# Linear attention and an MLP on one core: maxima of q and k subtracted on GpSimd for batches 4 to 7, with these batches' steps in other slots

## The chip, the cores and the metric

The kernel runs on one core of one Trainium2 chip. The core has five engines, each with its own instruction queue that is worked off in order: TensorE (PE, with its weight loads as PEld), VectorE (DVE), ScalarE (ACT), GpSimd (POOL) and SyncE (SP), which here issues most of the DMAs. The metric is the device time of one execution in microseconds (us), of which the median over several runs is taken.

## What is computed

The reference is a linear attention, followed by an MLP with a leaky activation:

```python
q_s = q - np.max(q, axis=-1, keepdims=True)          # q, k, v: 8 x 8 x 576 x 64
q_s = np.exp(q_s)
q_s = q_s / (np.sum(q_s, axis=-1, keepdims=True) + 1e-09)
k_s = k - np.max(k, axis=2, keepdims=True)
k_s = np.exp(k_s)
k_s = k_s / (np.sum(k_s, axis=2, keepdims=True) + 1e-09)
kv = np.einsum('bhsd,bhse->bhde', k_s, v)
a = np.einsum('bhsd,bhde->bhse', q_s, kv)

x = a.transpose(0, 2, 1, 3).reshape(4608, 512)
h = x @ w_in                                         # 512 x 2048
g = np.maximum(0.01 * h, h)
out = g @ w_out                                      # 2048 x 512
```

## The kernel before

**Tiles.** The 4608 tokens are nine tiles of 512, and the attention has eight batches of 576 tokens. Batch b's attention has to be ready ahead of the tile that first needs its tokens, so the attention of later batches is worked in between the matmuls of earlier tiles. The last two tiles are treated in another way (fewer products from sums of weights, which DVE and GpSimd form in `out_weight_sums` and `in_weight_sums`, L825); the change doesn't touch them.

**A plain tile** has two layers on PE. Layer 1 (L563) is 16 groups of four matmuls of 128x512; each group fills one PSUM bank `ph` out of a pool of six, and ACT's `leaky` (L572, out `gj`) empties it. Layer 2 (L584) is four token blocks of 16 matmuls; each block fills one of two banks `pout`, and ACT copies it to `out_sb` (L578), from where SP stores it. The six banks are also those of the attention.

**Slots.** The order of everything else is written by hand: `at(t, u, ...)` hangs functions in slot u of tile t. Slots 0 to 15 come after the groups of layer 1, slots 16 to 31 in layer 2, one after each four matmuls; a slot of 32 or more counts on into the next tile. What a slot issues is appended to the queues of its engines, so the slots fix each engine's order.

**The steps of a batch b**, with the names and lines that the profile shows. q and k are 128 partitions x 2304 elements (4 pairs of heads, 9 rows, 64), in f32, in a pool of six buffers shared with v:

- `load_all` (L84): SP's DMAs of k, q and v.
- `k_tree` (L160): DVE, four maxima over the rows of k, out `t` and `kmax`; in `k_max` of the plan.
- `k_allmax` (L167 to L190): DVE, the maximum over the partitions, out `kall`.
- `k_sub` (L198): k less its maximum, on the engine that it is given; `k_exp` (L206): ACT, out `ke`.
- `q_max` (L245): DVE; `q_sub` (L304): q less its maximum, on the engine that it is given; `q_exp` (L312): ACT, out `qe`.
- `q_sum` (L321, with the reciprocal L323) and `q_norm` (L328): DVE, together `q_ready`; `q_turn` (L551): a transposing DMA in SP's queue, out `qX`.
- `v_cast` (L216 on ACT, L218 on GpSimd): v to bf16, out `vb`.
- `attend_kv(b)`: PE interleaves the product of keys and values of batch b + 1 (L341) with the attention of batch b (L479) in six banks `pokv` and `po`. DVE's `kd_make(b + 1)` (L361, L362) follows, and then ACT's six copies to `xT` (L500), the last two of which read the banks `pokv` that `kd_make` reads, too. `kd` of b + 1 is what attends the next batch.

`k_tree`, `k_allmax`, `q_max`, `q_sum` and `q_norm` are DVE's in all batches from 2 on; GpSimd subtracts only for parts of batches 0 to 2 in the kernel before. `q_front(b, t, u)` of the plan stands for `q_max` and `q_sub(nc.vector, ...)`.

Of the kernel before, what the change touches and what calls it, by code (L numbers as in the profile page):

```python
# [26 lines left out]
def kernel(  # L27
# [9 lines left out]
    nc = tc.nc  # L37
# [52 lines left out]
    ALLH, ALLR = slice(0, HL), slice(0, R)  # L90
# [71 lines left out]
    def k_allmax(b):  # L162
        k_lanes(b)
        k_cross(b)

    def k_lanes(b):
        nc.vector.transpose(  # L167
            out=st[b]["kmaxT"], in_=st[b]["kmax"].rearrange("p h d -> p (h d)")
        )
        st[b]["m2"] = m2 = small_pool.tile([P, CB, 2], FP32, name="m2")  # L170
        nc.vector.tensor_reduce(
            out=m2[:, :, 0],
            in_=st[b]["kmaxT"].rearrange("p (c j) -> p c j", j=32),
            axis=AX.X,
            op=ALU.max,
        )

    def k_cross(b):
        m2 = st[b]["m2"]
        for a in range(4):  # L180
            o = a ^ 1
            nc.vector.tensor_reduce(
                out=m2[32 * o : 32 * o + 32, :, 1],
                in_=m2[32 * a : 32 * a + 32, :, 0:1],
                axis=AX.X,
                op=ALU.max,
            )
        m = small_pool.tile([P, CB], FP32, name="m")
        nc.vector.tensor_reduce(out=m, in_=m2, axis=AX.X, op=ALU.max)
        nc.vector.transpose(  # L190
            out=st[b]["kall"].rearrange("p h d -> p (h d)"),
            in_=m.unsqueeze(2).to_broadcast([P, CB, 32]),
        )

    def k_sub(eng, b, hs):
        ks = st[b]["k"][:, hs]
        n = hs.stop - hs.start
        eng.tensor_tensor(  # L198
            out=ks,
            in0=ks,  # L200
            in1=st[b]["kall"][:, hs].unsqueeze(2).to_broadcast([P, n, R, D]),
            op=ALU.subtract,
        )

    def k_exp(b, hs):
        nc.scalar.activation(  # L206
            out=st[b]["ke"][:, :, hs].rearrange("p r h d -> p h r d"),
            in_=st[b]["k"][:, hs],
            func=AF.Exp,
        )  # L210
# [10 lines left out]
    def q_cols(b, rs, hs):  # L221
        if b != 1:
            return st[b]["qe"][:, rs, hs]
        blocks = XE if rs.start else XH[hs.start // 2]
        return qe1[:, blocks].rearrange("p n c -> p (n c)").rearrange(
            "p (r h d) -> p r h d", h=hs.stop - hs.start, d=D
        )

    def turned(name):
        return qT_pool.tile([P, XE.stop, P], BF16, name=name, tag="qT")  # L230
# [11 lines left out]
    def q_max(b, rs, hs=ALLH):  # L242
        n, m = rs.stop - rs.start, hs.stop - hs.start
        st[b]["qmax", rs.start, hs.start] = o = small_pool.tile([P, HL, n], FP32, name="qmax")[:, 0:m]
        nc.vector.tensor_reduce(out=o, in_=st[b]["q"][:, hs, rs], axis=AX.X, op=ALU.max)  # L245
# [55 lines left out]
    def q_sub(eng, b, rs, hs=ALLH):  # L301
        n, m = rs.stop - rs.start, hs.stop - hs.start
        qs = st[b]["q"][:, hs, rs]
        eng.tensor_tensor(  # L304
            out=qs,
            in0=qs,
            in1=st[b]["qmax", rs.start, hs.start].unsqueeze(3).to_broadcast([P, m, n, D]),
            op=ALU.subtract,
        )

    def q_exp(b, rs, hs=ALLH):
        nc.scalar.activation(  # L312
            out=q_cols(b, rs, hs).rearrange("p r h d -> p h r d"),
            in_=st[b]["q"][:, hs, rs],
            func=AF.Exp,
        )
# [19 lines left out]
    def kv_quads(b, gg, outs, rs=ALLR):  # L336
        for r in range(R)[rs]:
            for hp in range(2):
                for hh in range(2):
                    rows = slice(hh * L, (hh + 1) * L)  # L340
                    nc.tensor.matmul(  # L341
                        outs[hh][hp * D : (hp + 1) * D, 0 : D + 1],
                        lhsT=st[b]["ke"][rows, r, 2 * gg + hp],
                        rhs=vb2[b % 2][rows, r, gg, hp, 0 : D + 1],
                        start=(r == 0),
                        stop=(r == R - 1),
                    )
# [139 lines left out]
    def attend(b, ggs, rows, pool=psB_pool, tag=BANK_TAG):  # L487
        n = (rows.stop - rows.start) * L
        ps = [pool.tile([P, len(ggs), n], FP32, name="po", tag=tag) for _ in range(2)]
        for i, gg in enumerate(ggs):  # L490
            cross(b, gg, [ps[hp][:, i] for hp in range(2)], rows)
        st[b]["po", ggs, rows.start] = ps
# [11 lines left out]
    def attend_kv(b, rows=R7, rest=RE):  # L504
        n = 2 * (rest.stop - rest.start) * L
        both = [psB_pool.tile([P, n + 2 * (D + 2)], FP32, name="pokv", tag=BANK_TAG) for _ in range(2)]
        ps = [a[:, 0:n].rearrange("p (g c) -> p g c", g=2) for a in both]
        st[b + 1]["pkv"] = pkv = [a[:, n:].rearrange("p (g d) -> p g d", g=2) for a in both]
        part = lambda gg, r0, r1: kv_quads(b + 1, gg, [pkv[hh][:, gg] for hh in range(2)], slice(r0, r1))
        part(0, 0, 6)  # L510
        attend(b, (0,), rows)
        part(0, 6, R)
        part(1, 0, 3)
        attend(b, (1,), rows)
        part(1, 3, R)
        for gg in range(2):
            cross(b, gg, [ps[hp][:, gg] for hp in range(2)], rest)
        keep = [lambda gg=gg, hp=hp: x_keep(nc.scalar, b, (gg,), rows, hp) for gg in range(2) for hp in range(2)]
        st[b]["po", (0, 1), rest.start] = ps
        kd_make(b + 1)  # L520
        for fn in keep:
            fn()
        for hp in range(2):
            x_keep(nc.scalar, b, (0, 1), rest, hp)
# [23 lines left out]
    def q_turn(b, rs=ALLR):  # L548
        if rs.start == 0:
            st[b]["qX"] = turned("qX")[:, 0 : 2 * R]  # L550
        nc.sync.dma_start_transpose(  # L551
            out=st[b]["qX"][:, 2 * rs.start : 2 * rs.stop],
            in_=st[b]["qe"][:, rs].rearrange("p r h d -> p (r h d)"),
        )
# [40 lines left out]
    def at(t, u, *fns):  # L595
        while t > 0 and u >= 32:
            t, u = t + 1, u - 32
        hooks.setdefault((t, u), []).extend(fns)
# [7 lines left out]
    def load_all(b, order="kqv"):  # L606
        for name in order:
            cuts = [(H0, ALLR), (H1, ALLR)] if b == B - 1 or (b, name) in ((B - 2, "q"), (B - 2, "v")) else [(ALLH, ALLR)]
            st[b][name] = load(dict(q=q, k=k, v=v)[name], b, f"{name}_raw", cuts)
# [134 lines left out]
    def q_front(b, t, u):  # L744
        at(t, u, lambda: q_max(b, ALLR), lambda: q_sub(nc.vector, b, ALLR))
# [19 lines left out]
    def k_max(b, t, u):  # L765
        at(t, u, lambda: k_begin(b), lambda: q_begin(b), lambda: k_tree(b, ALLH))

    def k_less(b, t, u):
        at(t, u, lambda: k_allmax(b), lambda: k_sub(nc.vector, b, ALLH))

    def q_ready(b, t, u):
        at(t, u, lambda: q_sum(b, ALLR), lambda: q_norm(b, ALLR))

    def casts_act(b, *slots):
        for gg, (t, u) in enumerate(slots):
            at(t, u, lambda gg=gg: v_cast(nc.scalar, b, gg))

    q_front(4, 2, 20)
    k_max(5, 2, 28)
    at(2, 30, lambda: q_exp(4, ALLR))  # L780
    q_ready(4, 2, 30)
    casts_act(5, (3, 4), (3, 8))
    at(3, 8, lambda: q_turn(4), lambda: load_all(6, "kvq"))
    k_less(5, 3, 8)
    at(3, 14, lambda: k_exp(5, ALLH))
    q_front(5, 3, 14)
    at(3, 18, lambda: attend_kv(4))
    k_max(6, 3, 19)
    at(3, 20, lambda: q_exp(5, ALLR))
    q_ready(5, 3, 20)  # L790
    casts_act(6, (3, 28), (3, 30))
    at(3, 22, lambda: load_all(7, "kv"))
    at(3, 31, lambda: q_turn(5), lambda: load_all(7, "q"))
    k_less(6, 3, 31)
    at(4, 4, lambda: k_exp(6, ALLH))
    q_front(6, 4, 4)
    at(4, 9, lambda: q_exp(6, ALLR))
    k_max(7, 4, 9)
    q_ready(6, 4, 9)
    casts_act(7, (4, 16), (4, 16))  # L800
    at(4, 17, lambda: attend_kv(5))
    k_less(7, 4, 18)
    at(4, 18, lambda: q_turn(6))
    at(4, 22, lambda: k_exp(7, ALLH))
    q_front(7, 4, 24)
    at(4, 28, lambda: attend_kv(6))
    at(5, 0, lambda: q_exp(7, ALLR))
    at(5, 0, lambda: out_weight_tiles(), lambda: out_weight_sums("v1"))
    q_ready(7, 5, 0)
    at(5, 9, lambda: q_turn(7))  # L810


    TA, TB = NT - 2, NT - 1
# [706 lines left out]
```

## Time and profile before

| what | us |
|---|---|
| median of three runs (276.83 to 277.02) | 276.88 |
| the profiled execution | 277.08 |
| its span in the profile | 275.0 |
| PE busy | 266.7 |
| DVE busy | 225.1 |
| ACT busy | 184.5 |
| GpSimd (POOL) busy | 78.6 |

Times in the views are microseconds from the start of the span, durations of one instruction in groups are nanoseconds. A row of a timeline gives start, duration, engine, line, operation, out<-in, shape and count; a row of grouped instructions gives the count, then busy time and mean of one, and behind the second bar the engine's idle time ahead of them with what ended it. A timeline's row of several instructions runs from the start of the first to the end of the last.

### The profile page before, as it was taken

To read this page: it belongs to the slowest core of one execution; us is meant where nothing else is said; L and a number is where in the kernel's file an instruction comes from. 1 tells how busy PE (TensorE), PEld (TensorE's weight loads), DVE (VectorE), ACT (ScalarE), POOL (GpSimd) and SP (SyncE) were. 2 spreads that over 40 slices of the span, in tenths; PEclk is the share of its full clock that TensorE was granted. 3 is DMA by queue.
4 is the path that set the end of the run, shared out by engine and by line. 5 is a ranking of instruction groups with operands and counts; after the bars stand their busy time and mean duration, and the time that the engine had idled before them with its cause. 6 is when DMAs were issued, how large, how long until landed. Compare 5 with 4: busy or idle time off the path is not lost.

```text
span 275.0 us, 5446 instructions
## 1 busy us (share of the span) xinstructions
PE 266.7 (97%) x2090; PEld 162.8 (59%) x2114; DVE 225.1 (82%) x330; ACT 184.5 (67%) x336; POOL 78.6 (29%) x97
## 2 busy tenths in 40 slices
PE   8799999999999999999999999999999999999994
PEld 3378644444444554454445444466676777889994
DVE  2995995999999999978999995989945757669962
ACT  3977573785389368986699569657746767984241
POOL 2866470149103000000000910000002999950000
PEclk9999999999999999999999999999999999999999
DMA  6999999987997699597991631400033000025254
GB/s 233 338 210 318 245 274 261 391 278 238 241 380 281 76 334 341 108 384 226 374 228 49 126 79 38 86 4 0 2 76 76 0 4 0 0 52 117 64 115 115
DMA packets 40569, 46.48 MB, mean 169 GB/s; under 512 B 18912, under 2 KB 24288, under 8 KB 40544
## 3 DMA queue, kind: packets, MB, share of 16 engines
q1 hardware_dynamic: 36720, 41.56, 51.2%
q0 software_dynamic: 3504, 4.20, 8.8%
q10 hardware_dynamic: 320, 0.39, 0.4%
q8 instruction: 16, 0.26, 0.4%
q14 instruction: 9, 0.07, 0.1%
HBM read 36.70 MB, written 9.44 MB: 168 GB/s over the span
## 4 chain that ended last, share of the span: by engine, by line
PE 93%; DVE 3%; DMA 2%; issue 1%; ACT 0%; SPq 0%
PE ph L563 35%; PE pout L584 25%; PE pout L1095 10%; PE pq L1344 10%; PE pp L1063 9%; DMA k_raw<-in_k_dram 2%; PE po L479 2%; DVE t L160 1%; PE pokv L341 1%; PE pkv L341 1%; PE pkv L419 0%; DVE k_raw L410 0%; ACT ke L206 0%; DVE kmax L160 0%; DVE kd L434 0%
## 5 line engine op out<-in xcount | busy, mean ns | idle before, releaser
L563 PE MATMUL ph<-xT,w_in_sb 128*128 128x512 bf16 (+1 forms) x503 | 98.9, 352 | 0.5
L563 PEld LDWEIGHTS <-w_in_sb 128*128 128x128 bf16 x512 | 49.5, 98 | 46.0 <-issue 0.2
L584 PE MATMUL pout<-w_out_sb,gj 128*128 128x512 bf16 x309 | 70.1, 379 | 1.1 <-issue 0.8
L572 ACT ACTIVATE gj<-ph 128x512 bf16<-128x512 f32 x88 | 49.2, 606 | 14.0 <-PE ph L563 13.0
L584 PEld LDWEIGHTS <-gj 128*128 128x128 bf16 x320 | 30.6, 98 | 36.2 <-issue 0.4
L825 POOL TENSOR_TENSOR t<-w_in_sb 128x256 fp32r<-128x256 bf16 x16 | 11.1, 693 | 62.1 <-ACT vb L216 62.1
L321 DVE TENSOR_REDUCE qsum<-qe 128x36 f32<-128x2304 bf16 (+5 forms) x13 | 20.0, 1542 | 4.7 <-ACT qe L312 4.5
L206 ACT ACTIVATE ke<-k_raw 128x2304 bf16<-128x2304 f32 (+2 forms) x13 | 18.0, 1383 | 6.1 <-DVE k_raw L198 5.7
L328 DVE TENSOR_TENSOR qe<-qe,qrec 128x2304 bf16<-128x2304 bf16 (+5 forms) x13 | 21.5, 1656 | 0.4
L578 ACT COPY out_sb<-pout 128x512 f32<-128x512 f32 x16 | 9.5, 591 | 17.9 <-PE pout L584 13.4
L245 DVE TENSOR_REDUCE qmax<-q_raw 128x36 f32<-128x2304 f32 (+5 forms) x13 | 20.0, 1537 | 0.4 <-DMA q_raw<-in_q_dram 0.4
L312 ACT ACTIVATE qe<-q_raw 128x2304 bf16<-128x2304 f32 (+5 forms) x13 | 17.2, 1326 | 4.2 <-POOL q_raw L304 3.2
L198 DVE TENSOR_TENSOR k_raw<-k_raw,kall 128x1152 f32<-128x1152 f32 (+2 forms) x10 | 18.0, 1820 | 0.3
L572 ACT ACTIVATE xT<-ph 128x512 bf16<-128x512 f32 x24 | 13.9, 600 | 6.3 <-PE ph L563 6.0
L304 POOL TENSOR_TENSOR q_raw<-q_raw,qmax 128x512 f32<-128x512 f32 (+3 forms) x7 | 11.8, 1680 | 20.7 <-DVE qmax L245 19.2
L1260 DVE COPY u<-pp 128x512 f32<-128x512 f32 x8 | 5.5, 691 | 13.5 <-PE pp L1063 13.5
L500 ACT CAST xT<-po 128x448 bf16<-128x448 f32 (+3 forms) x31 | 13.2, 510 | 3.4 <-PE po L479 3.4
L1289 POOL COPY gate<-u 128x1 f32<-128x1 f32 x1 | 0.2, 187 | 52.5 <-DVE u L1066 52.5
L218 POOL CAST vb<-v_raw 128x1152 bf16<-128x1152 f32 x7 | 9.8, 1435 | 17.3 <-DMA v_raw<-in_v_dram 17.3
L1063 PE MATMUL pp<-s,t 128*128 128x512 f32 x48 | 13.9, 398 | 0.0
L304 DVE TENSOR_TENSOR q_raw<-q_raw,qmax 128x2304 f32<-128x2304 f32 (+1 forms) x6 | 13.2, 2203 | 0.2
L825 POOL TENSOR_TENSOR t<-w_in_sb,t 128x256 fp32r<-128x256 bf16 x16 | 13.1, 818 | 0.6
(169 smaller groups left out, 441.9 us busy)
## 6 DMA issues: line engine op xcount, KB each, us to landing
out_dram<-out_sb SPq DMA_DIRECT2D x60, 128.0 KB, 3.0
k_raw<-in_k_dram SPq DMA_DIRECT2D x8, 576.0 KB, 5.7
v_raw<-in_v_dram SPq DMA_DIRECT2D x8, 576.0 KB, 7.6
q_raw<-in_q_dram SPq DMA_DIRECT2D x4, 1152.0 KB, 9.3
v_raw<-in_v_dram SPq DMA_DIRECT2D x4, 1152.0 KB, 11.4
k_raw<-in_k_dram SPq DMA_DIRECT2D x4, 1152.0 KB, 6.2
q_raw<-in_q_dram SPq DMA_DIRECT2D x4, 576.0 KB, 6.9
w_in_sb<-in_moe_w_in_dram POOLq DMA_DIRECT2D x7, 256.0 KB, 6.8
```

What stands on the lines that cost most here:

```text
L198: eng.tensor_tensor(out=ks, in0=ks, in1=st[b]["kall"][:, hs].unsqueeze(2).to_broadcast([P, n, R, D]), op=ALU.subtract,)
L245: nc.vector.tensor_reduce(out=o, in_=st[b]["q"][:, hs, rs], axis=AX.X, op=ALU.max)
L304: eng.tensor_tensor(out=qs, in0=qs, in1=st[b]["qmax", rs.start, hs.start].unsqueeze(3).to_broadcast([P, m, n, D]), op=ALU.subtract,)
L321: nc.vector.reduce_sum(out=qsum, in_=q_cols(b, rs, hs), axis=AX.X)
L328: nc.vector.tensor_tensor(out=qes if out is None else out, in0=qes, in1=st[b]["qrec", rs.start, hs.start].unsqueeze(3).to_broadcast([P, n, ...
L563: nc.tensor.matmul(ph, lhsT=w_in_sb[:, cb, j * P : (j + 1) * P], rhs=xT[:, cb, c0 : c0 + n], start=(cb == 0 and first), stop=(cb == NB - 1 ...
L572: nc.scalar.activation(out=o, in_=ph, func=AF.Prelu, alpha=LEAKY_SLOPE)
L584: nc.tensor.matmul(pout, lhsT=g_sb[j // 2][:, j % 2, tsub * P : (tsub + 1) * P], rhs=w_out_sb[:, j, os], start=(j == 0), stop=(j == NF - 1),)
L825: eng.tensor_tensor(out=late[o], in0=a, in1=b, op=ALU.subtract)
L1063: nc.tensor.matmul(ps, lhsT=w(c), rhs=a(c), start=(first and c == 0), stop=(c == 1), skip_group_check=True)
L1095: nc.tensor.matmul(ps[:, i], lhsT=a(m)[:, i * P : (i + 1) * P], rhs=w(m), start=(first and m == 0 and i == 0), stop=(m == NH - 1 and i == ...
L1344: nc.tensor.matmul(ps[i], lhsT=a(m)[:, i * P : (i + 1) * P], rhs=w(m), start=(first and m == 0 and (each or i == 0)), stop=(m == NH - 1 an ...
```

## The change

The q and k subtractions of batches 4 to 7 go to GpSimd, except that of k of batch 4, which stays on DVE. `q_less(b)` replaces `q_front(b)`: the same `q_max` on DVE, then `q_sub` on GpSimd. `k_all(b)` replaces `k_less(b)`: the same `k_allmax` on DVE, then `k_sub` on GpSimd. All slots of these batches but some are new: the maxima of k of batch 5 are issued at slot (2,22) rather than (2,28), so ahead of `attend_kv(3)` at (2,27) rather than behind it; those of batches 6 and 7 at (3,13) and (3,27) rather than (3,19) and (4,9). `attend_kv(4)` and `attend_kv(5)` keep their slots, `attend_kv(6)` goes from (4,28) to (4,23), and the last transposition of q from (5,9) to (4,25). The loads of k and v of batch 6 come ahead of the transposition of q of batch 4. Lines of the changed kernel behind the plan are four further on (L825 is L829).

```diff
-    def k_less(b, t, u):
-        at(t, u, lambda: k_allmax(b), lambda: k_sub(nc.vector, b, ALLH))
-
@@
-    q_front(4, 2, 20)
-    k_max(5, 2, 28)
+    def q_less(b, t, u):
+        at(t, u, lambda: q_max(b, ALLR), lambda: q_sub(nc.gpsimd, b, ALLR))
+
+    def k_all(b, t, u):
+        at(t, u, lambda: k_allmax(b), lambda: k_sub(nc.gpsimd, b, ALLH))
+
+    q_less(4, 2, 20)
+    k_max(5, 2, 22)
+    k_all(5, 2, 30)
     at(2, 30, lambda: q_exp(4, ALLR))
     q_ready(4, 2, 30)
+    at(3, 3, lambda: load_all(6, "kv"))
     casts_act(5, (3, 4), (3, 8))
-    at(3, 8, lambda: q_turn(4), lambda: load_all(6, "kvq"))
-    k_less(5, 3, 8)
-    at(3, 14, lambda: k_exp(5, ALLH))
-    q_front(5, 3, 14)
+    at(3, 6, lambda: k_exp(5, ALLH))
+    q_less(5, 3, 6)
+    at(3, 9, lambda: q_turn(4), lambda: load_all(6, "q"))
+    k_max(6, 3, 13)
+    at(3, 16, lambda: q_exp(5, ALLR))
+    k_all(6, 3, 17)
     at(3, 18, lambda: attend_kv(4))
-    k_max(6, 3, 19)
-    at(3, 20, lambda: q_exp(5, ALLR))
-    q_ready(5, 3, 20)
-    casts_act(6, (3, 28), (3, 30))
-    at(3, 22, lambda: load_all(7, "kv"))
-    at(3, 31, lambda: q_turn(5), lambda: load_all(7, "q"))
-    k_less(6, 3, 31)
-    at(4, 4, lambda: k_exp(6, ALLH))
-    q_front(6, 4, 4)
-    at(4, 9, lambda: q_exp(6, ALLR))
-    k_max(7, 4, 9)
-    q_ready(6, 4, 9)
-    casts_act(7, (4, 16), (4, 16))
+    q_ready(5, 3, 19)
+    at(3, 20, lambda: load_all(7, "kv"))
+    casts_act(6, (3, 20), (3, 22))
+    at(3, 22, lambda: k_exp(6, ALLH))
+    q_less(6, 3, 22)
+    at(3, 26, lambda: q_turn(5), lambda: load_all(7, "q"))
+    k_max(7, 3, 27)
+    at(4, 1, lambda: q_exp(6, ALLR))
+    k_all(7, 4, 1)
+    q_ready(6, 4, 1)
+    casts_act(7, (4, 5), (4, 7))
+    at(4, 8, lambda: k_exp(7, ALLH))
+    q_less(7, 4, 8)
+    at(4, 11, lambda: q_turn(6))
+    at(4, 16, lambda: q_exp(7, ALLR))
     at(4, 17, lambda: attend_kv(5))
-    k_less(7, 4, 18)
-    at(4, 18, lambda: q_turn(6))
-    at(4, 22, lambda: k_exp(7, ALLH))
-    q_front(7, 4, 24)
-    at(4, 28, lambda: attend_kv(6))
-    at(5, 0, lambda: q_exp(7, ALLR))
+    q_ready(7, 4, 18)
+    at(4, 23, lambda: attend_kv(6))
+    at(4, 25, lambda: q_turn(7))
     at(5, 0, lambda: out_weight_tiles(), lambda: out_weight_sums("v1"))
-    q_ready(7, 5, 0)
-    at(5, 9, lambda: q_turn(7))
```

## The prediction

> **What bounds the kernel now.** I read the page first: busy time, the slices, and the chain of work that ended last.
>
> ```profile
> span 275.0 us, 5446 instructions
> PE 266.7 (97%) x2090; PEld 162.8 (59%) x2114; DVE 225.1 (82%) x330; ACT 184.5 (67%) x336; POOL 78.6 (29%) x97
> PE   8799999999999999999999999999999999999994
> POOL 2866470149103000000000910000002999950000
> PE 93%; DVE 3%; DMA 2%; issue 1%; ACT 0%; SPq 0%
> ```
>
> TensorE (PE) is the chain. GpSimd (POOL) is empty from about 90 to 150 us, DVE is not. The next view gives the waits of PE, the one after it busy time in the stretches that the change touches (columns: length, then PE, PEld, DVE, ACT, POOL, then clock, DMA share and GB/s).
>
> ```profile
> PE pout L584 <- issue: 0.8, 5, 0.2
> 95.00:122.00 27.00, 26.89 (x214) 12.46 (x217) 26.16 (x30) 21.19 (x31) 0.00 (x0) 1.00 0.92 279
> 122.00:150.00 28.00, 27.74 (x213) 13.01 (x216) 25.16 (x29) 22.21 (x33) 0.00 (x0) 1.00 0.78 241
> 150.00:165.00 15.00, 14.68 (x233) 7.60 (x235) 14.56 (x21) 9.52 (x19) 7.70 (x8) 1.00 0.47 94
> ```
>
> PE is short of full by 0.11, 0.26 and 0.32 us there, at full clock. So nothing that DVE is spared can bring more than these 0.7 us, and of them only the gaps of 0.2 us behind an attention stretch could close. DVE, at 26.16 of 27.00 us, is close to a second bound, and that matters for the loss: what delays DVE delays ACT, which empties the PSUM banks that PE fills.
>
> **The change, part by part.** Seven subtractions (q of batches 4 to 7, k of 5 to 7; 128x2304 f32) leave DVE for GpSimd, and the steps of these batches move to earlier slots. Removed from DVE, and the nearest rows for their price on GpSimd:
>
> ```profile
> L304 DVE TENSOR_TENSOR q_raw<-q_raw,qmax 128x2304 f32<-128x2304 f32 x5 | 12.8, 2558 | 0.2
> L198 DVE TENSOR_TENSOR k_raw<-k_raw,kall 128x2304 f32<-128x2304 f32 x4 | 10.2, 2558 | 0.2
> L304 POOL TENSOR_TENSOR q_raw<-q_raw,qmax 128x512 f32<-128x512 f32 x3 | 3.1, 1040 | 14.6 <-DVE qmax L245 14.3 <-DVE krec L430 0.3
> L304 POOL TENSOR_TENSOR q_raw<-q_raw,qmax 128x1536 f32<-128x1536 f32 x1 | 2.8, 2758 | 1.2 <-ACT qe L312 1.2
> L825 POOL TENSOR_TENSOR t<-w_in_sb 128x256 fp32r<-128x256 bf16 x16 | 11.1, 693 | 62.1 <-ACT vb L216 62.1
> L932 POOL TENSOR_TENSOR 6r<-6r,gj 128x512 fp32r<-128x512 f32 x2 | 2.3, 1182 | 0.0
> ```
>
> DVE is spared 7 x 2.56 = 17.9 us. For q the line through 1040 ns at 512 and 2758 ns at 1536 elements (1.68 ns each, 0.18 us fixed) gives 4.05 us at 2304. In k's subtraction the second operand changes with each element, as in the last two rows: (1182 - 693)/256 = 1.91 ns each gives 1.18 + 1792 x 1.91 ns = 4.6 us, and 1182 ns in plain proportion 5.3 us. I take 4.05 for q and 4.7 for k; the bounds are 3.7 to 4.4 (a tenth each way) for q, 4.05 to 5.06 for k. The Trainium skill ("GPSIMD Engine Reference", section 3.1) gives 4497 ns for 2048 such elements; worked out for 2304 that is an estimate of 5.06 us for every one of the seven, and by it the sum below would be 12.5 us; for q the two rows above contradict it.
>
> Far more than the price counts what runs beside it, for DVE and GpSimd appear to hold each other up:
>
> ```profile
> 55.51 2.76 POOL L304 TENSOR_TENSOR q_raw<-q_raw,qmax 128x1536 f32<-128x1536 f32 x1 [1.16 <-ACT qe L312]
> 57.66 1.82 DVE L198 TENSOR_TENSOR k_raw<-k_raw,kall 128x1152 f32<-128x1152 f32 x1
> L198 DVE TENSOR_TENSOR k_raw<-k_raw,kall 128x1152 f32<-128x1152 f32 x5 | 7.1, 1444 | 0.1
> 154.65 2.56 DVE L198 TENSOR_TENSOR k_raw<-k_raw,kall 128x2304 f32<-128x2304 f32 x1
> 154.80 2.93 POOL L825 TENSOR_TENSOR t<-w_in_sb,t 128x256 fp32r<-128x256 bf16 x1
> ```
>
> The POOL row that ends at 58.27 overlaps the DVE row from 57.66, which takes 1.82 us, 0.4 over the mean of 1.44: about what is left of the 0.6 overlapped. In the other direction the POOL row from 154.80 takes 2.93 us in place of some 0.7, ending 0.5 after DVE's at 157.21. So I read a lock held for the whole instruction: an operation of DVE with two inputs in SBUF waits until GpSimd's ends, and the reverse; reductions go on. No row shows a DVE operation held for over 0.9 us; a whole GpSimd subtraction must be extrapolated. The Trainium skill ("SBUF — State Buffer", section "SBUF: two separate sides") says that whichever of the two starts first has the shared port pair for the entire instruction and the other blocks fully; the two overlaps agree, and by it the extrapolation holds; without it the sum would be near zero (first rival).
>
> I then followed the new order of each engine's queue forward from 97.7 us, each instruction starting when its engine, its inputs and the lock allow. The rows with the starts and durations, first DVE's (the two of 111.84 and 113.65 are the first and last of seven of the cross-lane maximum, 2.3 us in all):
>
> ```profile
> 97.73 2.54 DVE L245 TENSOR_REDUCE qmax<-q_raw 128x36 f32<-128x2304 f32 x1
> 102.79 0.16 DVE L361 RECIPROCAL krec<-pokv 128x2 f32<-128x2 f32 x1
> 103.59 1.22 DVE L160 TENSOR_TENSOR t<-k_raw 128x1024 f32<-128x1024 f32 x1
> 104.84 1.15 DVE L160 TENSOR_TENSOR t<-t 128x512 f32<-128x512 f32 x2
> 106.03 0.42 DVE L160 TENSOR_TENSOR kmax<-t,k_raw 128x256 f32<-128x256 f32 x1
> 111.84 0.44 DVE L167 STREAM_TRANSPOSE kmaxT<-kmax 128x256 f32<-128x256 f32 x1
> ...
> 113.65 0.45 DVE L190 STREAM_TRANSPOSE kall<-m 128x256 f32<-128x256 f32 x1
> ```
>
> Then ACT's, where a row of several gives the pitch (2.24/4 and 2.21/2, less some 0.06 of overlap), and the exponentials:
>
> ```profile
> 103.36 0.78 ACT L500 CAST xT<-pokv 128x256 bf16<-128x256 f32 x2
> 104.04 2.13 ACT L312 ACTIVATE qe<-q_raw 128x2304 bf16<-128x2304 f32 x1
> 106.53 0.61 ACT L572 ACTIVATE gj<-ph 128x512 bf16<-128x512 f32 x1
> 115.27 2.24 ACT L572 ACTIVATE gj<-ph 128x512 bf16<-128x512 f32 x4
> 119.13 2.12 ACT L206 ACTIVATE ke<-k_raw 128x2304 bf16<-128x2304 f32 x1
> 131.63 2.21 ACT L216 CAST vb<-v_raw 128x1152 bf16<-128x1152 f32 x2
> ```
>
> Then the load of k of batch 5 (issue, and time to landing) and PE:
>
> ```profile
> 95.03 0.58 SPq L84 DMA_DIRECT2D k_raw<-in_k_dram x1
> k_raw<-in_k_dram SPq DMA_DIRECT2D x1, 1152.0 KB, 6.1
> ```
>
> ```profile
> 105.43 13.98 PE L563 MATMUL ph<-xT,w_in_sb 128*128 128x512 bf16 x63
> 160.84 0.38 PE L341 MATMUL pokv<-vb,ke 64*64 64x65 bf16 x24
> ```
>
> A layer 1 of PE is 16 groups in 13.98 us: 0.86 us each, over six banks.
>
> *A, layer 1 of tile 3.* GpSimd takes q of batch 4 at 100.34 and keeps the lock to 104.4. The tree of k maxima of batch 5 now stands on DVE ahead of the kd of batch 4. Its data land at 95.03 + 6.1 = 101.1, but the lock holds it to 104.3; with 1.22 + 1.15 + 0.42 us it ends at 107.0. kd, at 102.79 before, follows at 107.0. Behind kd wait ACT's copy of the attention banks (103.36, now 107.5) and, in ACT's queue, q's exponential (108.2 to 110.3) and the first activation of tile 3 (106.53, now 110.7, ended at 111.3). PE's seventh group needs that bank at 105.6 + 6 x 0.86 = 110.8: it stands 0.54 us. From there ACT runs without a pause, 0.50 us an activation, with a cast of 1.05 or an exponential of 2.02 between them: two more waits, 0.51 and 0.31 us. A = 1.4 us.
>
> *B, layer 2 of tile 3.* k of batch 5 goes on GpSimd from 109.85 to 114.55, so DVE's q normalization waits from 113.3 to 114.4, the next q maximum ends at 119.5, and the first tree operation of batch 6 at 120.6. There GpSimd's waiting q of batch 5 slips in (120.5 to 124.5); the tree, the cross-lane maximum (some 2.2 us) and k's subtraction of batch 6 end at 126.0, 128.0 and 132.8. ACT has q's exponential ahead of the attention copies, then k's exponential ahead of layer 2's output copies, which free the two output banks: PE waits 0.78 and 2.30 us. B = 3.1 us.
>
> *C, layer 1 of tile 4.* The same again: q of batch 6 splits the tree of batch 7 (138.7 to 142.8), k of batch 7 runs from 146.3 to 151.0, its exponential stands ahead of the activations, and PE's sixteenth group waits 1.9 us. C = 1.9 us.
>
> *D, the moved attention.* Batch 6 is attended five slots sooner. q of batch 7 on GpSimd ends at 160.1, its exponential stands on ACT ahead of batch 5's copies, and the six banks that batch 6 needs come free 0.3, 0.3, 0.3 and 0.1 us late. D = 1.0 us.
>
> Nothing: the moved loads and transpositions in SP's queue, and GpSimd's queue. On SP, k and v of batch 6 now stand ahead of the transposition of q of batch 4; v's buffer is free after the q exponential of batch 4 (110.3), while the transposition waits anyway for the normalization (114.4 to 117.0), and a k issued near 108.5 lands well ahead of 119.4, where its tree begins (9 us later it would cost 0.3). On GpSimd, the eight sums of weights stand behind the seventh subtraction, hidden by some 50 us until they are next wanted (the slices show GpSimd empty again to about 210). Sum: 1.4 + 3.1 + 1.9 + 1.0 = 7.4 us. The same bookkeeping with the order of before gives PE no wait in this stretch, which is what its row shows.
>
> The profiled run took 277.08 us (span 275.0 and 2.1 around it), 0.2 above the median of 276.88. On the median: 284.2.
>
> **The rivals.** *No slower: GpSimd does not hold DVE.* The 1.82 us row may be chance; only DVE holding GpSimd is shown over 2 us. It decides at the first place, 101.1 us: if the tree of batch 5 starts there, it ends at 103.9, kd at 104.7 in place of 103.7, ACT is 1 us late and has that back in the slack of six banks; every later k and q is ready sooner than needed. All of A to D fall away: 276.9. Against it speaks that both overlaps fit one rule.
>
> *DVE keeps the lock through its tree.* If GpSimd cannot enter between two dependent DVE operations, the trees of batches 6 and 7 end 4 us sooner and q's subtractions come later by 1.6. A stays; B becomes 2.2 + 1.2 = 3.4, C 0.4, D 1.0: 6.2 us, 283.1 (with k at 4.05 us 4.9, 281.8). No row shows a GpSimd operation waiting through such a chain; the gaps of some 0.03 us between tree operations speak for entering.
>
> *GpSimd is dearer.* With q at 4.4 and k at 4.9 us A is 1.7, B 3.8, C 2.4 and D 1.4: 9.3 us, 286.2. *Cheaper*, q at 3.7 and k at 4.05: 1.0 + 1.4 + 1.15 + 0.65 = 4.2 us, 281.1.
>
> *Faster.* The three gaps of 0.16 us that follow the attention stretches close, and DVE is early everywhere: 276.4. Nothing in the trace names what ends these gaps but issue.
>
> **How the numbers follow.** Chances: the forecast 0.45 (its own range, k from 4.05 to 5.06 us: 5.7 to 8.4, 282.5 to 285.3), the lock kept through the tree 0.25, dearer 0.10, cheaper 0.10, no hold 0.08, faster 0.02. Of no hold I count 0.06 as within 0.2% (0.55 us, about what a measurement of this kernel can tell) and 0.02 as slower. So faster 0.02, same 0.06, slower 0.92. The range leaves out the no-hold case and half of the dearer and the cheaper one: 280.6 to 286.6.
>
> **What would show it.** Right: GpSimd's subtractions near 4.05 and 4.7 us when not held themselves; the tree of batch 5 starting near 104.3, not 101.1; kd of batch 4 at about 107; PE waiting on ACT's activations in tile 3's layer 1, on its output copies at the end of tile 3, and in layer 1 of tile 4; PE's busy time unchanged. Wrong: DVE's two-input operations starting inside a GpSimd subtraction; PE without a wait on ACT; the tree of batch 6 unbroken (the second rival); or a wait on a DMA, which I price at nothing.

## The result and the profile after

| | median, us | range | ratio to before (95% interval) |
|---|---|---|---|
| before | 276.86 | 276.67 to 277.02 | |
| changed | 287.35 | 286.21 to 288.94 | 1.0383 (1.0333 to 1.0434) |
| changed, measured again | 286.83 | 286.15 to 287.22 | 1.0358 (1.0339 to 1.0378) |

The change makes the kernel 10.0 to 10.5 us slower; 7.4 were forecast, and the time lies above the range. From the page of the first profile (execution of 288.94 us), the slices in the same columns as before, and from its waits of PE:

```profile
span 287.1 us, 5484 instructions
PE 272.6 (95%) x2114; PEld 164.2 (57%) x2114; DVE 222.8 (78%) x323; ACT 184.4 (64%) x336; POOL 109.1 (38%) x104
PE   7799999999999999997696999999999999999994
POOL 2856460159003053367346660000000899970000
PEclk9779999999999999999999799999999999999999
...
PE pout L584 <- ACT out_sb L578: 4.1, 2, 2.5
PE ph L563 <- ACT gj L572: 3.1, 3, 2.4
```

Two things are new in it. PE waits 7.2 us for ACT, in layer 1 (L572) and for the output banks (L578); before it waited for neither. And the row PEclk, all 9 before, has two dips. The busy time by stretch of the same execution shows them in the column after POOL, the granted clock:

```profile
12.00:16.00 4.00, 4.00 (x26) 2.09 (x26) 2.61 (x8) 2.72 (x3) 3.59 (x6) 0.50 1.12 212
157.00:160.00 3.00, 2.06 (x5) 0.71 (x5) 3.00 (x2) 3.00 (x7) 0.00 (x0) 0.59 0.35 66
160.00:163.00 3.00, 3.00 (x80) 1.52 (x82) 0.13 (x1) 0.82 (x2) 2.74 (x1) 0.84 0.70 131
```

The first dip lies ahead of all that the change touches (tile 0's first group starts at 18.03 us rather than 15.67, so this one execution is 2.4 us late there); the second follows PE's longest wait in layer 1. To read the steps of the prediction without them, I use the profile of an execution of the same kernel in which the clock stayed at 1.00 throughout: 286.15 us, span 284.3 (`after_again` below). Its busy time in the three stretches shown of before:

```profile
95.00:122.00 27.00, 25.67 (x199) 11.78 (x200) 25.27 (x29) 19.77 (x31) 11.09 (x3) 1.00 0.94 282
122.00:150.00 28.00, 23.71 (x191) 11.00 (x191) 27.12 (x32) 18.74 (x27) 15.04 (x4) 1.00 0.85 234
150.00:165.00 15.00, 12.37 (x138) 5.82 (x139) 9.39 (x9) 10.06 (x15) 9.91 (x7) 1.00 0.22 41
```

PE lacks 1.33, 4.29 and 2.63 us there, where it lacked 0.11, 0.26 and 0.32; and DVE, spared 17.9 us of subtractions, is as full as before until 150. What it does with that time the timelines of GpSimd and DVE in this execution show:

```profile
100.06 4.05 POOL L304 TENSOR_TENSOR q_raw<-q_raw,qmax 128x2304 f32<-128x2304 f32 x1 [11.31 <-issue]
109.95 5.06 POOL L198 TENSOR_TENSOR k_raw<-k_raw,kall 128x2304 f32<-128x2304 f32 x1 [5.84 <-DVE kall L190]
120.02 4.91 POOL L304 TENSOR_TENSOR q_raw<-q_raw,qmax 128x2304 f32<-128x2304 f32 x1 [5.01 <-ACT gj L572]
```

```profile
100.80 4.39 DVE L160 TENSOR_TENSOR t<-k_raw 128x1024 f32<-128x1024 f32 x1 [0.87 <-DMA k_raw<-in_k_dram]
106.75 0.16 DVE L361 RECIPROCAL krec<-pokv 128x2 f32<-128x2 f32 x1
113.16 4.27 DVE L328 TENSOR_TENSOR qe<-qe,qrec 128x2304 bf16<-128x2304 bf16 x1
119.81 1.21 DVE L160 TENSOR_TENSOR t<-k_raw 128x1024 f32<-128x1024 f32 x1
121.06 4.88 DVE L160 TENSOR_TENSOR t<-t 128x512 f32<-128x512 f32 x2
```

It waits. The first tree operation of batch 5 takes 4.39 us in place of 1.22: it ends 1.08 us after GpSimd's subtraction, which ends at 104.11. A normalization of 2.56 us takes 4.27 beside k's subtraction. And GpSimd's q of batch 5, queued at 120.02, gets in when the first tree operation of batch 6 ends at 121.0; the next two, 1.15 us before, take 4.88. The time that an instruction is held up stands in its duration, not in the idle time ahead of it, which is why the busy share of DVE hardly fell. kd of batch 4 comes at 106.75, and so the chain reaches ACT and PE:

```profile
107.33 0.78 ACT L500 CAST xT<-pokv 128x256 bf16<-128x256 f32 x2 [4.43 <-DVE krec L361]
110.49 2.57 ACT L572 ACTIVATE gj<-ph 128x512 bf16<-128x512 f32 x5
124.96 2.12 ACT L312 ACTIVATE qe<-q_raw 128x2304 bf16<-128x2304 f32 x1 [2.36 <-POOL q_raw L304]
134.00 2.12 ACT L206 ACTIVATE ke<-k_raw 128x2304 bf16<-128x2304 f32 x1 [1.39 <-POOL k_raw L198]
152.96 2.12 ACT L206 ACTIVATE ke<-k_raw 128x2304 bf16<-128x2304 f32 x1 [1.42 <-POOL k_raw L198]
162.02 2.12 ACT L312 ACTIVATE qe<-q_raw 128x2304 bf16<-128x2304 f32 x1 [3.52 <-POOL q_raw L304]
```

```profile
101.61 3.63 PE L584 MATMUL pout<-w_out_sb,gj 128*128 128x512 bf16 x15
105.08 5.34 PE L563 MATMUL ph<-xT,w_in_sb 128*128 128x512 bf16 x24
111.15 6.20 PE L563 MATMUL ph<-xT,w_in_sb 128*128 128x512 bf16 x27 [0.73 <-ACT gj L572]
117.70 3.05 PE L563 MATMUL ph<-xT,w_in_sb 128*128 128x512 bf16 x12 [0.35 <-ACT gj L572]
120.59 2.75 PE L584 MATMUL pout<-w_out_sb,gj 128*128 128x512 bf16 x12
130.56 3.61 PE L584 MATMUL pout<-w_out_sb,gj 128*128 128x512 bf16 x16 [1.60 <-ACT out_sb L578]
136.65 3.61 PE L584 MATMUL pout<-w_out_sb,gj 128*128 128x512 bf16 x15 [2.48 <-ACT out_sb L578]
155.62 1.02 PE L563 MATMUL ph<-xT,w_in_sb 128*128 128x512 bf16 x4 [2.41 <-ACT gj L572]
158.30 0.38 PE L341 MATMUL pokv<-vb,ke 64*64 64x65 bf16 x24
159.72 5.13 PE L584 MATMUL pout<-w_out_sb,gj 128*128 128x512 bf16 x23 [0.16 <-issue]
164.78 0.66 PE L341 MATMUL pokv<-vb,ke 64*64 64x65 bf16 x24
167.08 7.08 PE L584 MATMUL pout<-w_out_sb,gj 128*128 128x512 bf16 x31
```

Every wait of PE ends with ACT. ACT waited for kd (first row) ahead of tile 3's activations, and then for GpSimd: for q of batch 5 (124.96) and k of batch 6 (134.00) ahead of the two output copies of B, for k of batch 7 (152.96) ahead of C's activations, and for q of batch 7 (162.02) ahead of D's copies.

At an unbroken boundary PE's rows overlap by 0.16 us (101.61 + 3.63 against 105.08), so each listed wait is 0.16 less than what is lost. A third wait of A isn't listed: the 12 matmuls from 117.70 take 3.05 us, the 12 from 120.59 take 2.75. With that, by the prediction's letters: A 1.70 (0.89, 0.51 and 0.30; in the first profile the first of them is 0.50, and A 1.31), B 4.40, C 2.57. For D, the attention of batch 6 takes 164.78 to 167.08, 2.30 us. That of batch 5 shows 1.42, but its 0.16 us of "issue" is no wait: this profile has records of 2090 matmuls for 2114 weight loads, and the row from 159.72 has 23 of 24 matmuls. The first profile has all 2114, and there the same stretch takes 1.19 (162.10 to 163.29) with no such gap. So D is 1.1. The sum is 9.8. The spans differ by 9.3, since PE comes to tile 3 0.35 us sooner than before (105.08 against 105.43); 0.1 is left.

### The profile page after: what moved, and what is told of

Its sections match the earlier page's. It is cut to its first block, busy times and chain, and to the rows that moved or that the text cites. A ratio compares the mean times of both kernels' runs of the same rounds, so it can differ in the third digit from the quotient of the medians.

```text
span 287.1 us, 5484 instructions
## 1 busy us (share of the span) xinstructions
PE 272.6 (95%) x2114; PEld 164.2 (57%) x2114; DVE 222.8 (78%) x323; ACT 184.4 (64%) x336; POOL 109.1 (38%) x104
## 4 chain that ended last, share of the span: by engine, by line
PE 49%; issue 1%; ACT 0%; DVE 0%; ACTq 0%
PE ph L563 15%; PE pout L1099 9%; PE pq L1348 9%; PE pp L1067 9%; PE pout L584 6%; PE pokv L341 0%; PE po L479 0%; ACT gj L572 0%; DVE gu L1070 0%; PE pokv L479 0%; ACTq L572 0%
## 5 line engine op out<-in xcount | busy, mean ns | idle before, releaser
L563 PE MATMUL ph<-xT,w_in_sb 128*128 128x512 bf16 (+1 forms) x512 | 101.0, 354 | 3.2 <-ACT gj L572 3.1
L584 PE MATMUL pout<-w_out_sb,gj 128*128 128x512 bf16 x320 | 72.4, 382 | 4.1 <-ACT out_sb L578 4.1
L572 ACT ACTIVATE gj<-ph 128x512 bf16<-128x512 f32 x88 | 48.2, 609 | 11.0 <-PE ph L563 10.3
L304 POOL TENSOR_TENSOR q_raw<-q_raw,qmax 128x2304 f32<-128x2304 f32 (+4 forms) x11 | 29.7, 2699 | 50.4 <-DVE qmax L245 33.3
L328 DVE TENSOR_TENSOR qe<-qe,qrec 128x2304 bf16<-128x2304 bf16 (+5 forms) x13 | 26.8, 2061 | 0.4
L198 POOL TENSOR_TENSOR k_raw<-k_raw,kall 128x2304 f32<-128x2304 f32 (+1 forms) x4 | 17.4, 4359 | 13.8 <-DMA out_dram<-out_sb 5.8
L578 ACT COPY out_sb<-pout 128x512 f32<-128x512 f32 x16 | 9.2, 593 | 19.4 <-PE pout L584 13.4
L572 ACT ACTIVATE xT<-ph 128x512 bf16<-128x512 f32 x24 | 14.3, 597 | 7.8 <-PE ph L563 7.6
L160 DVE TENSOR_TENSOR t<-t 128x256 f32<-128x256 f32 (+2 forms) x22 | 17.3, 788 | 0.7
L160 DVE TENSOR_TENSOR t<-k_raw 128x512 f32<-128x512 f32 (+1 forms) x11 | 12.7, 1155 | 1.9 <-DMA k_raw<-in_k_dram 1.8
L502 DVE CAST xT<-po 128x256 bf16<-128x256 f32 (+2 forms) x5 | 2.6, 554 | 13.0 <-PE po L479 13.0
## 6 DMA issues: line engine op xcount, KB each, us to landing
out_dram<-out_sb SPq DMA_DIRECT2D x60, 128.0 KB, 2.8
```

Source lines behind the costliest of these rows:

```text
L160: nc.vector.tensor_tensor(out=o, in0=i0, in1=i1, op=ALU.max)
L304: eng.tensor_tensor(out=qs, in0=qs, in1=st[b]["qmax", rs.start, hs.start].unsqueeze(3).to_broadcast([P, m, n, D]), op=ALU.subtract,)
L328: nc.vector.tensor_tensor(out=qes if out is None else out, in0=qes, in1=st[b]["qrec", rs.start, hs.start].unsqueeze(3).to_broadcast([P, n, ...
L563: nc.tensor.matmul(ph, lhsT=w_in_sb[:, cb, j * P : (j + 1) * P], rhs=xT[:, cb, c0 : c0 + n], start=(cb == 0 and first), stop=(cb == NB - 1 ...
L572: nc.scalar.activation(out=o, in_=ph, func=AF.Prelu, alpha=LEAKY_SLOPE)
L584: nc.tensor.matmul(pout, lhsT=g_sb[j // 2][:, j % 2, tsub * P : (tsub + 1) * P], rhs=w_out_sb[:, j, os], start=(j == 0), stop=(j == NF - 1),)
```

## The experiments

Theory Q: the new slots put long steps of the front ahead of what PE waits for, and the lock between DVE and GpSimd makes these steps longer. Its numbers come from the same bookkeeping as the prediction's, with k's subtraction at its measured 5.06 us. Its rivals were E (the engine alone), S (the slots alone) and N (no lock, only GpSimd's slowness).

**Slots without the engine.**

```diff
-        at(t, u, lambda: q_max(b, ALLR), lambda: q_sub(nc.gpsimd, b, ALLR))
+        at(t, u, lambda: q_max(b, ALLR), lambda: q_sub(nc.vector, b, ALLR))
-        at(t, u, lambda: k_allmax(b), lambda: k_sub(nc.gpsimd, b, ALLH))
+        at(t, u, lambda: k_allmax(b), lambda: k_sub(nc.vector, b, ALLH))
```

> The new slots, with all seven subtractions back on VectorE. Theory Q (queue order: the new slots put long steps of the front ahead of what PE waits for, and the lock between VectorE and GpSimd lengthens them): the same bookkeeping as in the prediction gives waits of PE of 2.7 and 1.2 us for the output banks at the end of tile 3 and 1.5 us at the attention of batch 6, none in layer 1: 5.4 us, 0.2 more for each restart, so about 282.9, and 284.6 if the granted clock drops once after the long wait. Rival E (the engine alone: GpSimd's slower subtractions and its lock are the whole loss): no wait, 277. Rival S (the slots alone): the waits of the changed kernel stay, 286 to 287.

283.95 us, ratio 1.0259 (1.0242 to 1.0277). With nothing on GpSimd the slots alone cost 7.1 us. DVE, ACT and PE of this kernel at the end of tile 3:

```profile
127.12 2.56 DVE L198 TENSOR_TENSOR k_raw<-k_raw,kall 128x2304 f32<-128x2304 f32 x1
129.60 0.16 DVE L361 RECIPROCAL krec<-pokv 128x2 f32<-128x2 f32 x1
...
130.17 0.77 ACT L500 CAST xT<-pokv 128x256 bf16<-128x256 f32 x2 [4.29 <-DVE krec L361]
...
131.49 8.34 PE L584 MATMUL pout<-w_out_sb,gj 128*128 128x512 bf16 x31 [3.55 <-ACT out_sb L578]
```

The tree, the maximum and the subtraction of batch 6 now stand on DVE ahead of kd of batch 5; behind kd stand ACT's copies, and behind those the output copy that frees PE's bank. One wait of 3.5 us rather than two of 2.7 and 1.2, and 0.6 us listed at the attention of batch 6 rather than 1.5; the mechanism is theory Q's, and the time lies between its 282.9 and 284.6. Neither rival comes near.

**The engine without the slots.** In the kernel before, only the engine of the seven subtractions:

```diff
-        at(t, u, lambda: k_allmax(b), lambda: k_sub(nc.vector, b, ALLH))
+        at(t, u, lambda: k_allmax(b), lambda: k_sub(nc.gpsimd, b, ALLH))
-    q_front(4, 2, 20)
+    def q_less(b, t, u):
+        at(t, u, lambda: q_max(b, ALLR), lambda: q_sub(nc.gpsimd, b, ALLR))
+
+    q_less(4, 2, 20)
-    q_front(5, 3, 14)
+    q_less(5, 3, 14)
...
```

> The slots of the kernel before, with the seven subtractions on GpSimd. Theory Q: one wait of 3.6 us at the end of tile 4, where the late attention copies hold up the output copies, and nothing before: 280.7, and 282.4 if the clock drops after it. Rival E: the whole loss, 286 to 287. Rival S: 277.

283.37 us, 1.0233 (1.0211 to 1.0254): one wait, of 4.1 us, where theory Q put it (it had 3.6), and a clock that falls behind it. The time is 1.0 us over the 282.4 expected with a drop of the clock. The engine alone costs 6.5 us, the slots alone 7.1, both together 10.0 to 10.5: neither is the whole, and they don't add up.

**q alone, k alone**, in the new slots (one of the two edits of the first experiment each).

> The new slots with only q's four subtractions on GpSimd, k's three on VectorE. Theory Q: 1.4 us in layer 1 of tile 3 as with the full change, 4.1 and 1.2 at its end, 0.4 in layer 1 of tile 4, 3.6 at the attention of batch 6: 10.7 us, so 288.6 with the restarts, 290.3 with one drop of the clock; slower than the full change although three slow subtractions are taken off GpSimd. Rival E: between before and after by the share of GpSimd's time (16.2 of 31.4 us), about 282. Rival S: 286 to 287.

> The new slots with only k's three subtractions on GpSimd, q's four on VectorE. Theory Q: no wait at the start of tile 3, 2.4 us for an output bank at its end, 1.0 in layer 1 of tile 4, nothing at the attention of batch 6: 3.4 us, so 280.7, 282.4 with one drop of the clock. Rival E: by GpSimd's time about 282. Rival S: 286 to 287.

290.36 us (1.0488; 1.0473 to 1.0504) and 281.93 us (1.0185; 1.0169 to 1.02). q on GpSimd with k on DVE is 3 us slower than the full change although GpSimd does less, and k alone is 2 us faster than the slots with nothing on GpSimd. No cost that each subtraction adds can give this order; the order of the queues does. By itself k's 281.93 doesn't decide, since rival E had about 282, too. The wait of 1.0 us that was expected for k alone in layer 1 of tile 4 did not show; a drop of the clock stood ahead of it in this profile and may have covered it. Two executions of k alone at clock 1.00 take 281.94 and 282.18 us, the two at 0.994 take 281.71 and 281.93: here the drop costs nothing in the end.

**The lock by itself.** The kernel before, plus GpSimd subtractions that nobody reads, started by the same maxima:

```diff
+    def beside(m):
+        nc.gpsimd.tensor_tensor(out=scratch, in0=w_in_sb[...], in1=m, op=ALU.subtract)
...
-        at(t, u, lambda: k_allmax(b), lambda: k_sub(nc.vector, b, ALLH))
+        at(t, u, lambda: k_allmax(b), lambda: beside_k(b), lambda: k_sub(nc.vector, b, ALLH))
-        at(t, u, lambda: q_max(b, ALLR), lambda: q_sub(nc.vector, b, ALLR))
+        at(t, u, lambda: q_max(b, ALLR), lambda: b > 3 and beside_q(b), lambda: q_sub(nc.vector, b, ALLR))
```

> The kernel before, with seven further GpSimd subtractions of 128x1536 (w_in less qmax or kall, into a scratch tile that nobody reads), each released by the same maximum as the ones that the change moves; VectorE keeps all of its own. Theory Q with the lock: each takes some 3.0 us, VectorE's next operation with two SBUF inputs waits until it ends, and by the bookkeeping PE waits 0.6 and 2.9 us at the end of tile 4: 280.7, up to 282.4 with a drop of the clock. Rival N (GpSimd holds nobody up; what costs is that GpSimd's subtraction comes later than VectorE's): nothing waits for the added ones, 276.9.

282.79 us, 1.0213 (1.0191 to 1.0235), with waits of 1.2 and 2.9 us at the end of tile 4. Rival N falls: nothing depends on these instructions. Both directions show in the first of them, on GpSimd and DVE of this kernel:

```profile
100.45 5.14 POOL L768 TENSOR_TENSOR scratch<-w_in_sb,qmax 128x1536 bf16<-128x1536 bf16 x1 [11.30 <-DVE qmax L245]
...
100.40 2.56 DVE L304 TENSOR_TENSOR q_raw<-q_raw,qmax 128x2304 f32<-128x2304 f32 x1
103.68 2.98 DVE L160 TENSOR_TENSOR t<-k_raw 128x1024 f32<-128x1024 f32 x1
```

GpSimd stands until DVE's subtraction ends at 102.96 and then runs to 105.59; DVE's tree operation is held until then and ends 1.07 us later.

**Where the subtraction is free.** Slots of before, GpSimd for q of batches 4, 5 and 7 and k of batch 5 only:

```diff
-        at(t, u, lambda: k_allmax(b), lambda: k_sub(nc.vector, b, ALLH))
+        at(t, u, lambda: k_allmax(b), lambda: k_sub(nc.gpsimd if b in (5,) else nc.vector, b, ALLH))
...
+        at(t, u, lambda: q_max(b, ALLR), lambda: q_sub(nc.gpsimd if b in (4, 5, 7) else nc.vector, b, ALLR))
```

> The slots of the kernel before, with four of the seven subtractions on GpSimd: q of batches 4, 5 and 7, k of batch 5. Theory Q: VectorE waits for the lock at each, but what it delays has that much slack in the old slots; no wait of PE, 276.9 within 0.3. Rival E (each subtraction on GpSimd costs its share): 4/7 of the 6.5 us that all seven cost in the old slots, 280.6.

277.0 us, 1.0007 (0.9997 to 1.0016): the same as before, with one wait of 0.5 us for an exponential of k that was not expected. Four subtractions of 4 to 5 us on GpSimd cost nothing to be measured; rival E falls. They gain nothing either. Not each of them holds DVE, as theory Q had it: beside the first a tree operation takes 2.91 us in place of 1.22, beside the last a sum of weights 3.03 in place of 2.29, and beside the other two DVE has a maximum to do or waits for PE.

**Is the late kd the root?** Only the tree of batch 5 back behind it:

```diff
-    k_max(5, 2, 22)
+    k_max(5, 2, 28)
```

> The changed kernel with the tree of batch 5 at (2,28) again, behind kd of batch 4, everything else as changed. Theory Q: kd is at about 103 again, ScalarE's first activation of tile 3 is 4 us sooner, the two waits in its layer 1 shrink from 1.0 to 0.4 us, those at its end and in tile 4 stay: 0.7 us less than the changed kernel, 286 to 287. Rival (the late kd makes all that follows late): the later waits shrink with it, under 284.

286.11 us, 0.7 under the 286.83 of the changed kernel, as theory Q has it. kd of batch 4 starts here at 101.97 rather than 106.75:

```profile
101.97 0.17 DVE L361 RECIPROCAL krec<-pokv 128x2 f32<-128x2 f32 x1 [2.03 <-PE pokv L479]
```

The first of A's waits goes, the waits of B and C stay at 1.60, 2.48 and 2.42 us: they have their own causes.

**Are the exponentials only in the wrong place?**

```diff
-    at(3, 22, lambda: k_exp(6, ALLH))
+    at(3, 31, lambda: k_exp(6, ALLH))
-    at(4, 8, lambda: k_exp(7, ALLH))
+    at(4, 15, lambda: k_exp(7, ALLH))
```

> The changed kernel with the exponentials of k of batches 6 and 7 later on ScalarE, (3,31) for (3,22) and (4,15) for (4,8), so that the output copies and the activations are ahead of them. Theory Q: the wait of 2.5 us for the second output bank and that of 2.4 us at the sixteenth group go, but the front is as late as before, so that a wait of 2.3 us in layer 1 of tile 4 behind q's exponential and one of 3.6 us at the attention of batch 6 come instead; the sum stays 8.4 us, 286 to 288. Rival (the two waits are the fault of where these exponentials stand, and end there): 4.9 us and the drop of the clock less, 281 to 282.5.

287.85 us. The waits of 2.5 and 2.4 us are gone as expected, and waits of 2.05 us in layer 1 of tile 4 and 1.3 at the attention of batch 6 have come instead (2.3 and 3.6 were expected). The whole front is late; moving one step moves the wait.

**The sooner attention of batch 6.**

```diff
-    at(4, 23, lambda: attend_kv(6))
-    at(4, 25, lambda: q_turn(7))
+    at(4, 28, lambda: attend_kv(6))
+    at(5, 9, lambda: q_turn(7))
```

> The changed kernel with the attention of batch 6 back at (4,28) and the transposition of q of batch 7 at (5,9), as before. Theory Q: the bookkeeping has no wait at the attention then, but one of 2.3 us for an output bank ahead of it, since the output copies now stand behind q's exponential of batch 7, in place of 1.0 us; so 1 to 1.3 us slower than the changed kernel, 287.5 to 288.5, less what a drop of the clock covers. Rival (the sooner attention is what costs): 1 us faster, 285 to 286.

289.2 us: 2.4 us more than the changed kernel, in the direction of theory Q and 1.1 more than it had, so D is not a loss against the old slot. The trace also shows what a drop of the clock does; three of PE's waits in this kernel:

```profile
136.97 5.30 PE L584 MATMUL pout<-w_out_sb,gj 128*128 128x512 bf16 x15 [2.48 <-ACT out_sb L578]
155.96 1.02 PE L563 MATMUL ph<-xT,w_in_sb 128*128 128x512 bf16 x4 [0.73 <-ACT gj L572]
167.29 6.16 PE L584 MATMUL pout<-w_out_sb,gj 128*128 128x512 bf16 x20 [2.11 <-ACT out_sb L578]
```

Behind the first, a block that takes 3.61 us takes 5.30: 1.69 lost. But the next wait is 0.73 us, against 2.41 in the execution without a drop: 1.68 given back, since ACT is the later one anyway. Behind the last it falls again (mean clock 0.988), and no later wait gives that back. The last wait loses 2.3 us where D loses 1.1, which is the 1.2 us of theory Q; the other half of the 2.4 us is put down to the clock, which no run shows by itself.

**Does the wait lower the clock?** The engine without the slots again, with PE kept busy in its one long wait by matmuls that nobody reads:

```diff
+    def fill(n):
+        ps = psB_pool.tile([P, TT], FP32, name="fill", tag=BANK_TAG)
+        for _ in range(n):
+            nc.tensor.matmul(ps, lhsT=w_in_sb[:, 0, 0:P], rhs=w_in_sb[:, 0, 0:TT], start=True, stop=True)
+
+    at(4, 27, lambda: fill(16))
```

> The slots of the kernel before with the seven subtractions on GpSimd (283.4 us, one wait of 4.1 us at the end of tile 4, mean clock 0.988), and in that wait sixteen idle matmuls of 128x512 (3.5 us) into a spare bank, whose result nobody reads. Theory H (the wait itself lets the granted clock fall, and that costs some 2 us more): with PE busy through the wait the clock stays at 1.0, the wait is 0.7 us, and the time falls by 2 to 2.7 us to 280.7 to 281.4, though the work grew. Rival: the clock falls for another reason, or the time is lost elsewhere: 283 to 284, clock still under 0.99.

282.12 us, 1.25 less than without the extra work. Busy time by stretch, first without and then with the fill:

```profile
163.00:168.00 5.00, 3.73 (x92) 1.95 (x91) 0.00 (x0) 2.68 (x6) 4.92 (x5) 0.51 0.49 108
```

```profile
163.00:168.00 5.00, 4.16 (x102) 2.18 (x101) 1.08 (x5) 3.88 (x8) 4.92 (x5) 1.00 0.44 96
```

The clock behind the wait goes from 0.51 to 1.00, in all four executions to 0.997 or more, where it had been 0.988 to 0.994. So it is PE's idleness that lowers it here. The gain is less than the 2 to 2.7 us expected: PE then waits 0.7 us for a transposition of q, which it does not when the clock is low, and 0.5 us for an exponential of k at 122 us, ahead of the fill, which the edit does not explain.

**The changed kernel again, and with a fill** (ten such matmuls at slot (4,14), ahead of C's wait):

> The changed kernel itself once more. Its first profile lost 2.4 us to a low granted clock between 10 and 17 us, ahead of anything that the change touches. If that is a matter of the single execution, a profile without it shows five waits of 7 to 7.5 us in sum, one drop of the clock of 3.4 us after a long wait, and 286 to 287; if the change causes it, the low clock is there again in the head.

> The changed kernel with ten idle matmuls of 128x512 (2.2 us) in the wait ahead of the sixteenth group of tile 4, into a spare bank, result unread. Theory: the wait there falls from 2.4 to about 0.2 us and the clock does not drop behind it; PE then comes 1.5 us sooner to the attention of batch 6, and the wait of 1.0 us that the prediction had there and the trace did not show comes up. The time falls by 0.5 only, to about 286.5. Rival (the prediction's wait at the attention of batch 6 was wrong, not covered): no wait there, 285.5.

286.83 us for the kernel itself. The low clock of the head is a matter of the single execution: this profile doesn't have it. It has no drop at all, though its waits are the same, and it is the fastest of its four (286.15; the others, at 0.993 or 0.994, 286.56 to 287.22). With the fill 287.25 us: 0.4 more, where 0.5 less was expected. The wait fell to 0.26 us, and the attention of batch 6 takes 2.30 us, as without the fill:

```profile
156.06 1.02 PE L563 MATMUL ph<-xT,w_in_sb 128*128 128x512 bf16 x4 [0.26 <-ACT gj L572]
165.22 0.65 PE L341 MATMUL pokv<-vb,ke 64*64 64x65 bf16 x24
167.52 1.69 PE L584 MATMUL pout<-w_out_sb,gj 128*128 128x512 bf16 x6
```

On the clock this run says nothing, since the profiled executions of both kernels had none of it. On D it does: the wait is there in both profiles in which PE comes at full speed, and in the first profile, with the drop ahead of it (0.59 and 0.84, above), there is none.

## Why the prediction was right and where it failed

| step | forecast, us | at clock 1.00 | what the runs say |
|---|---|---|---|
| A | 1.4 | 1.70 | right; 1.31 in the first profile; tree5_later takes 0.7 away |
| B | 3.1 | 4.40 | right places, too small |
| C | 1.9 | 2.57 | right place, too small |
| D | 1.0 | 1.1 | right; none behind the drop of the clock |
| clock | none | none | it drops in most executions; its share of the time is open |
| sum | 7.4 | 9.8 | 9.3 by the spans, PE being 0.35 ahead at the start |

(276.88 and 7.4 make 284.3, not the 284.2 of the forecast.)

- **The lock** is as read from one overlap in each direction (0.6 and 2.4 us): DVE operations are held for 3 us and more (1.22 shown as 4.39), a GpSimd operation for 2.5 (`beside`), also where nothing depends on GpSimd's work. The rival without it, to which the prediction gave 0.08, is refuted. One of its signs has to be read otherwise: the tree of batch 5 was to start near 104.3, and its row starts at 100.80, inside GpSimd's subtraction, because the row holds the waiting, too. Its end at 105.19 and kd at 106.75 are as forecast (105.5 and 107.0).
- **Who gets the lock between DVE's tree operations**: GpSimd does, a gap of 0.04 us is enough (121.02 to 121.06); the rival that DVE keeps it is refuted by the row of 4.88 us.
- **The failed step is the length of GpSimd's chain in B and C: two of its terms were too short.** The places of the waits and what each waits for are right. GpSimd's rows at clock 1.00 from q of batch 5 on, behind the row of 120.02:

```profile
128.91 5.06 POOL L198 TENSOR_TENSOR k_raw<-k_raw,kall 128x2304 f32<-128x2304 f32 x1 [3.98 <-DVE krec L361]
138.98 4.91 POOL L304 TENSOR_TENSOR q_raw<-q_raw,qmax 128x2304 f32<-128x2304 f32 x1 [5.01 <-DVE qmax L245]
147.86 5.07 POOL L198 TENSOR_TENSOR k_raw<-k_raw,kall 128x2304 f32<-128x2304 f32 x1 [3.98 <-DVE kall L190]
```

  The first term is the price of k's subtraction: I took 4.7 us out of 4.05 to 5.06, and it is 5.06 or 5.07 three times (109.95, and the two above). By the same bookkeeping 5.06 gives 8.4 in place of 7.4. The second is what DVE does between the end of q's subtraction and the start of k's, the rest of the tree and the cross-lane maximum: I had 3.5 us (124.5 to 128.0, 142.8 to 146.3), and it is 3.98 both times, 1.0 us in all. The rows of before have 2.3 us for the maximum alone, the prediction's times only 2.0 (126.0 to 128.0). So k of batch 6 ends 1.2 us later than forecast (133.97 against 132.8) and k of batch 7 1.9 (152.93 against 151.0); B and C together are 2.0 longer than forecast.
- **The price was in the trace of before**, in a row of k's own subtraction on GpSimd that the prediction doesn't use:

```profile
36.87 1.19 DVE L328 TENSOR_TENSOR qe<-qe,qrec 128x896 bf16<-128x896 bf16 x1
37.07 2.25 POOL L198 TENSOR_TENSOR k_raw<-k_raw,kall 128x576 f32<-128x576 f32 x1
```

  By the lock, GpSimd stands until DVE's operation ends at 38.06 and works until 39.32: 1.26 us for 576 elements, which is an estimate of 5.04 for 2304. Of the rows that the prediction uses, 1182 ns in plain proportion, 5.3 us, was nearer than the slope that I preferred. The Trainium skill ("GPSIMD Engine Reference", section 3.1), whose estimate I set aside, has it right to 0.01 us for k; for q, whose second operand repeats along the row, its 5.06 is 1.0 too high, and the 4.05 of the line through two rows is right.
- **The 0.16 us by which a listed wait is shorter than what is lost** is no term that the prediction left out: its A was worked out as time lost, 0.54, 0.51 and 0.31, and the first profile has 0.50, 0.51 and 0.30.
- **There was no term for the clock.** The trace of before has no long wait of PE, so none could show. Behind a wait of 2.1 to 4.7 us the clock falls to 0.5 in most executions. The Trainium skill ("TensorE: Matmul & The Clock Gate", Part 1) says that an idle window of about 3.4 us throttles PE to half its clock and that the window runs free; the half and the variation between executions agree with the rows here, but waits of 2.1 and 2.5 us were enough. What it adds to the time is not settled. In the first profile the drop behind C's wait loses 1.5 us, and 1.1 come back at the attention of batch 6. Of `after_again`, the execution at 1.00 is 0.4 to 1.1 us faster than the others, but of k alone those at 1.00 are no faster. So the 1.2 us between 286.15 and the median of 287.35 are not shown to be the clock's.
- **Faster** had nothing to close: the profile of before, too, has 2090 records for 2114 weight loads, and the gaps of 0.16 us behind its attention stretches are of the kind that the first profile, with all records, doesn't have. No run was faster than before; with four subtractions on GpSimd and no harm done, the time is the same.

## What to carry to other kernels

Where PE was at 97% and waited for no other engine in the stretch that changed, what DVE was spared brought nothing in any of these runs; in such a kernel, ask instead what a move delays, and follow it through each in-order queue to the bank that PE needs. GpSimd and DVE are not two engines for elementwise work with two inputs in SBUF: GpSimd takes 4.05 to 5.06 us for what takes DVE 2.56, and holds DVE's operations of that kind for all of it, so such a move can pay at most where DVE has reductions or nothing to do. Look for the operation itself in the trace before you go by its neighbours, and take time that a lock holds off its duration first. When waits are summed, compare the starts of rows with those of before rather than add up the listed waits: a listed wait is too short by the overlap of two rows, a short one isn't listed, and a gap can be a missing record. Then check which later wait gives back what a low clock costs.

## What the hardware showed that I had not expected

- On GpSimd a subtraction of 128x2304 f32 takes 4.05 us where the second operand repeats along the row (q) and 5.06 where it changes with each element (k); on DVE both take 2.56.
- A profile counts the time that an instruction is held by the lock as busy: 1.22 us of work show as 4.39. A waiting GpSimd operation enters between two dependent DVE operations 0.04 us apart.
- The granted clock falls to 0.5 for some 3 us and more behind waits of PE of 2.1 to 4.7 us, but not in every execution of the same kernel; and the 1.7 us that this costs can come back whole in the next wait.
